# Agent attention with an expert layer, one core: score and routing products kept in program order behind the second-layer products, and a Square that waits for its buffer's transfer by step count

## The chip, the cores and the metric

The kernel runs on one core of a Trainium2 chip. Its time is the device time of one launch in microseconds (us); less is better. The engines are named as the profile names them: PE (TensorE, matrix products; its weight loads have a row of their own, PEld), DVE (VectorE), ACT (ScalarE), POOL (GpSimd) and SP (SyncE, which here only issues DMA transfers). Each engine works through its own list of instructions in order.

## The reference, cut to what matters

Four batches of 11456 tokens with 128 channels. A softmax over the keys pools the values into 49 agent rows, a softmax over the agents gives every token its attention output x. Then a layer with eight experts: each token goes to the expert with the largest cosine to x, through two matrix products with a Relu between, times its gate.

```python
a2k = sm(agents, k)          # softmax over the 11456 keys
agent_v = a2k @ v            # 49 x 128
q2a = sm(q, agents)          # softmax over the 49 agents
x = q2a @ agent_v            # what the experts see
...
logits = xn @ en.T / tau     # xn, en: normalised rows
expert_idx = np.argmax(logits, axis=1)
...
h = np.maximum(x[mask] @ w1[e], 0.0)
out[mask] = gate_w[mask, None] * (h @ w2[e])
```

## The kernel before, in words

Nearly all tokens of a batch choose one expert. The kernel picks that expert per batch, runs the layer densely for it, and mends the few strays at the end.

A **tile** is 512 tokens (128 partitions by 4 columns), a **unit** is two tiles; a batch has 12 units, the last of 192 tokens. The inner width of 1024 is cut into eight blocks of 128, so there are 184 **steps** a batch and 736 in all, one for each (batch, tile, block). A step is:

- `ffn_mm1`: two products of 512 columns into the PSUM tile `hp` (L723, L724; `gh` and `gl` are the high and low half of the first weights, folded with the attention's values, `tt` the transposed softmax weights of the tokens), then on ACT the Relu into `hh` (L727) and on DVE the remainder `hl` (L728). `hp` has four buffers, and one is free again when `hl` is done.
- `ffn_mm2`, for the step four earlier (`LAG = 4`): 12 products of 128 columns into `yp` (L745 to L747).

Between the steps, generators prepare what later steps need; they hand over after a number of steps, and the numbers in their calls say how many. For each unit of keys and of queries `split` makes two halves in 16 bits: a Square on ACT (L299), three small instructions on DVE for a scale, a scaled copy on ACT (L303) into the buffer `xs` (named `ks` or `qs`), two instructions on POOL (L304, L305), and a DMA that transposes `xs` into `xT` (`kT` or `qT`, L307, issued from SP). `xs` and `xT` have `XB = 5` buffers each, shared by keys and queries. `scores` (L316 to L318) makes 24 small products of a unit into `sp`. For queries follow, in `q_unit`: the exponential (L578), two 16-bit halves `e` on ACT (L582) and POOL (L583), a transposing DMA into `tt` (L591), and the **routing products** `rtp` (L600, L601, 16 a unit), from which ACT takes `rtg` and `rt`. Values of the next batch are multiplied into `avp` (L406).

The keys of batch b+1 are split while batch b runs its steps; units of keys come about every 12 steps, units of queries every 16.

The program's text is only a proposal: a scheduler then writes each engine's list, and it may move an instruction ahead of others that stand before it in the text when, by its own estimates, that one could start earlier; `tc.high_priority(200)` lets `ffn_mm1` go ahead. The list is fixed when the kernel is built. On the chip an engine then follows its list, and waits where the next entry's operands aren't ready.

Of the kernel before, what the change touches and what calls it, by code (L numbers as in the profile page):

```python
# [3 lines left out]

# [26 lines left out]
def kernel(ctx: ExitStack, tc: tile.TileContext, q, k, v, agents, emb, tau, w1, w2, out):  # L31
# [24 lines left out]
    XB = 5  # L56
# [28 lines left out]


    ffn_at = [None]
    units = {}

    def tshape(t):  # L90
# [199 lines left out]

    def split(kind, b, u, g):

        s = units[kind, b, u]
        p, n = ushape(u)
        sq = sm.tile([P, 1], F32, name="usq", tag=kind + "usq", bufs=3)[:p]
        xs = wk.tile([P, UJ, 2, D], F16, name=kind + "s", tag="xs", bufs=XB)
        act.activation(xs[:p, :n, 0], s[:p, :n], AF.Square, accum_out=sq)  # L299
        yield g  # L300
        hs = half_scale(sq, 14, kind + "u", 4, *([qbias] if kind == "q" else []))
        sc, iv = yield from hs
        act.activation(xs[:p, :n, 0], s[:p, :n], AF.Copy, scale=sc)  # L303
        pool.tensor_tensor(out=s[:p, :n], in0=s[:p, :n], in1=sc.unsqueeze(2).broadcast_to([p, n, D]), op=ALU.mult)  # L304
        pool.tensor_tensor(out=xs[:p, :n, 1], in0=s[:p, :n], in1=xs[:p, :n, 0], op=ALU.subtract)  # L305
        xT = wk.tile([P, 2 * UJ, P], F16, name=kind + "T", tag="xT", bufs=XB)
        sp.dma_start_transpose(out=xT[:, : 2 * n, :p], in_=xs[:p, :n].rearrange("p c h d -> p (c h d)"))  # L307
        return xT, iv

    def scores(b, u, xT):  # L310
        p, n = ushape(u)
        s = pss("sp")
        for c in range(n):
            o = s[:p, c * A : (c + 1) * A]
            hi, lo = xT[:, 2 * c, :p], xT[:, 2 * c + 1, :p]
            pe.matmul(out=o, lhsT=hi, rhs=a16[:, b, :A], start=True, stop=False)  # L316
            pe.matmul(out=o, lhsT=hi, rhs=a16[:, b, A:], start=False, stop=False)
            pe.matmul(out=o, lhsT=lo, rhs=a16[:, b, :A], start=False, stop=True)  # L318
        return s[:p, : n * A].rearrange("p (c a) -> p c a", a=A)


# [233 lines left out]
    def q_unit(b, u, g):  # L555
        bt = batches[b]
        p, n = ushape(u)
        while ("q", b, u) not in units:
            yield 1
        f32 = b == 0 and u < QF  # L560
        if f32:
            xT = pe_T(units["q", b, u], p, n)
            yield 1
            s = pss("sp")
            for c in range(n):
                pe.matmul(out=s[:p, c * A : (c + 1) * A], lhsT=xT[:, c * p : (c + 1) * p], rhs=aT_all[:, b, :], start=True, stop=True)
            spv = s[:p, : n * A].rearrange("p (c a) -> p c a", a=A)
            iv = SCALE
        else:
            xT, iv = yield from split("q", b, u, g[0])  # L570
            yield g[1]
            spv = scores(b, u, xT)
        mx = sm.tile([P, UJ], F32, name="qmx", tag="qmx")[:p, :n]
        dve.tensor_reduce(out=mx, in_=spv, axis=AX.X, op=ALU.max)
        e = wk.tile([P, UJ, A], F32, name="qe", tag="qe", bufs=LEAD)[:p, :n]
        dve.tensor_tensor(out=e, in0=spv, in1=mx.unsqueeze(2).broadcast_to([p, n, A]), op=ALU.subtract)
        yield g[2]
        act.activation(e, e, AF.Exp, scale=iv)  # L578
        yield g[3]
        e2 = e16[u % len(e16)]  # L580
        hi = e2[:p, :n, :A]
        act.copy(hi, e)  # L582
        (dve if f32 else pool).tensor_tensor(out=e2[:p, :n, LO : LO + A], in0=e, in1=hi, op=ALU.subtract)  # L583
        tt = wk.tile([P, UJ * P], F16, name="tt", tag="tt", bufs=LEAD + 2)
        if f32:
            tp = psh("tp").bitcast(F16)
            for c in range(n):
                pe.transpose(out=tp[:, c * p : (c + 1) * p], in_=e2[:p, c, :], identity=ident16[:p, :p])
            act.copy(tt[:, : n * p], tp[:, : n * p])
        else:  # L590
            sp.dma_start_transpose(out=tt[:, : n * p].rearrange("k (c p) -> k c p", p=p),  # L591
                                   in_=e2[:p, :n, :].rearrange("p c k -> p (c k)"))
        yield g[4]
        tts[b, u] = tt
        while not hasattr(bt, "r_hi"):
            yield 1
        s = (pss if ffn_at[0] else psh)("rtp")
        for c in range(n):
            o = s[:p, c * RW : (c + 1) * RW]
            pe.matmul(out=o, lhsT=tt[:, c * p : (c + 1) * p], rhs=bt.r_hi, start=True, stop=False)  # L600
            pe.matmul(out=o, lhsT=tt[:, c * p : (c + 1) * p], rhs=bt.r_lo, start=False, stop=True)  # L601
        gi = group_of[u]
        us = groups[gi]
        if u == us[0]:
            rtgs[b, gi] = (wk.tile([P, GC, E + 1], F32, name="rtg", tag="rtg", bufs=4),
                           wk.tile([P, GC], F32, name="quad", tag="quad", bufs=4))
        rtg, quad = rtgs[b, gi]
        c0 = ucol(u) - ucol(us[0])
        cs = slice(c0, c0 + n)
        if p < P:  # L610
            pool.memset(rtg[p:, cs], 1.0)
            pool.memset(quad[p:, cs], 1.0)
        sv = s[:p, : n * RW].rearrange("p (c w) -> p c w", w=RW)
        rt = wk.tile([P, UJ, A], F32, name="rt", tag="rt", bufs=1)[:p, :n]
        act.copy(rtg[:p, cs], sv[:, :, : E + 1])  # L615
        act.copy(rt, sv[:, :, E + 1 :])
        pool.tensor_tensor(out=rt, in0=rt, in1=e, op=ALU.mult)
        yield g[5]
        dve.tensor_reduce(out=quad[:p, cs], in_=rt, axis=AX.X, op=ALU.add)
        if u == us[-1]:  # L620
            spawn(route_group(b, gi, c0 + n), 1, half=True)
# [92 lines left out]
    def ffn_mm1(i):  # L714
        b, t, f = ffn_steps[i]
        bt = batches[b]
        u, w = unit_of(t)
        p, n = tshape(t)
        m = p * n
        tt = tts[b, u][:, w * TJ * P : w * TJ * P + m]  # L720
        hp = psh("hp")
        fs = slice(f * P, (f + 1) * P)
        pe.matmul(out=hp[:, :m], lhsT=bt.gh[:, fs], rhs=tt, start=True, stop=False)  # L723
        pe.matmul(out=hp[:, :m], lhsT=bt.gl[:, fs], rhs=tt, start=False, stop=True)  # L724
        hh = wk.tile([P, TJ * P], F16, name="hh", tag="hh", bufs=LAG + 2)
        hl = wk.tile([P, TJ * P], F16, name="hl", tag="hl", bufs=LAG + 2)
        act.activation(hh[:, :m], hp[:, :m], AF.Relu)  # L727
        dve.scalar_tensor_tensor(out=hl[:, :m], in0=hp[:, :m], scalar=0.0, in1=hh[:, :m], op0=ALU.max, op1=ALU.subtract)  # L728
        live[i] = (hh, hl)

    def ffn_mm2(i):

        b, t, f = ffn_steps[i]
        bt = batches[b]
        p, n = tshape(t)
        hh, hl = live.pop(i)
        if f == 0:
            yps[b, t] = psy("yp").rearrange("p (c d) -> p c d", d=D)
        yp = yps[b, t]

        for c in range(n):
            y = yp[:p, c, :]
            cs = slice(c * p, (c + 1) * p)
            last = f == NF - 1 and c == n - 1
            pe.matmul(out=y, lhsT=hh[:, cs], rhs=bt.w2h[:, f, :], start=(f == 0 and c == 0), stop=False, skip_group_check=True)  # L745
            pe.matmul(out=y, lhsT=hh[:, cs], rhs=bt.w2l[:, f, :], start=False, stop=False, skip_group_check=True)  # L746
            pe.matmul(out=y, lhsT=hl[:, cs], rhs=bt.w2h[:, f, :], start=False, stop=last, skip_group_check=True)  # L747

    def ffn_out(b, t):

# [181 lines left out]


    active = []
    now = [0]

    def spawn(g, at=0, half=False):
        t0 = now[0] + (now[0] % 2)
        active.append([t0 + 2 * at, g, 1 if half else 2])
# [71 lines left out]
    def keys():  # L1011
# [12 lines left out]
        for i, (at, kind, b, u) in enumerate(ops):  # L1024
# [4 lines left out]
            if kind == "k":  # L1029
                if not hasattr(batches[b], "blks"):  # L1030
                    k_start(b)
                spawn(k1_unit(b, u, (1, 7)))
            else:
                kb = batches[b].blks[0]
                if u == 0:
                    while kb.k1 < NU:
                        yield 1
                    yield from k_max(b, pss, 1)
                    yield 1
                spawn(k2_unit(b, u, pool, (3, 4)))  # L1040
                if u == NU - 1:
                    spawn(after_keys(b))
# [6 lines left out]
    def queries():  # L1049
        for b in range(B):  # L1050
            for u in range(NU):
                if b == 0 and u < LEAD:
                    continue
                for i in (b * NU + u, b * NU + u + 1):
                    unit_load(q, "q", i // NU, i % NU)
                spawn(q_unit(b, u, (1, 7, 1, 1, 6, 2)), 3)
                yield UT * NF if u < NU - 1 else NF

    def step2(i):
# [70 lines left out]
```

## Time and profile before

| | us |
|---|---|
| median of 3 runs (1103.6 to 1106.59) | 1105.27 |
| the profiled execution | 1101.58 |
| its span, first to last instruction | 1099.8 |
| PE busy, of 13878 products | 1019.3 (93%) |
| DVE busy | 770.5 (70%) |
| ACT busy | 724.2 (66%) |
| POOL busy | 580.1 (53%) |

The first 100 us load, and score batch 0's keys; the 736 steps then run from 101 us to the end. A row of the waits reads: engine, tile and line of the one that waited, arrow, engine, tile and line of the one it waited for, then total us, times and the longest. A row of the timeline reads: start, duration, engine, line, operation, output and inputs, and in brackets the idle time before it and who ended it. A row of windows reads: from and to, length, and for each engine its busy us and instructions, then the clock that was granted to PE as a share, the mean busy share of the DMA engines, and GB/s.

### The profile page before, as it was taken

The numbers are of one execution on the slowest core, as the hardware profiler recorded it, in microseconds if no ns is written. First come the engines' busy times: TensorE is split into PE (matmuls) and PEld (weight loads), VectorE is DVE, ScalarE is ACT, GpSimd is POOL, SyncE is SP. The second block draws the span as 40 slices with busy tenths as digits, with TensorE's granted clock in tenths as the row PEclk, the third lists the DMA queues.
The fourth block names the chain that finished last, engine by engine and source line by source line (L and its number), as shares of the span: only waits on it lengthen the run. The fifth ranks groups of instructions, "written<-read, shape, count | busy, mean of one in ns | idle before, by whom it ended". The sixth has DMA issues, their size and how long they took to land.

```text
span 1099.8 us, 33877 instructions
## 1 busy us (share of the span) xinstructions
PE 1019.3 (93%) x13878; PEld 809.8 (74%) x13878; DVE 770.5 (70%) x1779; ACT 724.2 (66%) x1406; POOL 580.1 (53%) x653
## 2 busy tenths in 40 slices
PE   7876979999998898999999988999999989999997
PEld 7764767777776777777777766777777767877776
DVE  5665757666786677766686766766677778777785
ACT  3456978777559787766648866675556856755553
POOL 2334998786516987764524985544321835532300
PEclk9777999999999999999999999999999999999999
DMA  9549899956339988744436997452113524631101
GB/s 335 151 100 280 182 227 233 229 167 119 85 66 282 231 189 188 167 117 89 94 82 225 224 229 144 92 110 69 31 41 138 100 61 119 123 83 40 42 30 35
DMA packets 283944, 152.63 MB, mean 139 GB/s; under 512 B 208315, under 2 KB 260619, under 8 KB 283787
## 3 DMA queue, kind: packets, MB, share of 16 engines
q1 hardware_dynamic: 270603, 126.98, 51.2%
q10 hardware_dynamic: 13120, 23.47, 5.9%
q8 instruction: 109, 1.79, 0.7%
q14 instruction: 48, 0.39, 0.1%
q0 software_dynamic: 64, 0.00, 0.0%
HBM read 75.80 MB, written 23.53 MB: 90 GB/s over the span
## 4 chain that ended last, share of the span: by engine, by line
PE 53%; DMA 13%; POOL 13%; issue 9%; ACT 6%; DVE 5%; SPq 1%; ACTq 0%; POOLq 0%; DVEq 0%
PE hp L723 9%; PE yp L745 8%; PE yp L747 8%; PE hp L724 8%; PE yp L746 8%; DMA kT<-ks 4%; DMA tt<-e 4%; PE avp L406 4%; DMA qt<-in_q_dram 3%; POOL qs L305 2%; POOL qt L304 2%; POOL ks L305 2%; ACT hh L727 2%; POOL kt L304 2%; PE sp L380 2%
## 5 line engine op out<-in xcount | busy, mean ns | idle before, releaser
L728 DVE SCALAR_TENSOR_TENSOR hl<-hp,hh 128x512 f16<-128x512 f32 (+1 forms) x736 | 480.8, 671 | 142.5 <-ACT hh L727 121.7
L727 ACT ACTIVATE hh<-hp 128x512 f16<-128x512 f32 (+1 forms) x736 | 416.8, 588 | 186.1 <-PE yp L746 78.8
L745 PE MATMUL yp<-w2h,hh 128*128 128x128 f16 (+1 forms) x2880 | 522.4, 220 | 9.1 <-ACT hh L727 8.1
L746 PE MATMUL yp<-w2l,hh 128*128 128x128 f16 (+1 forms) x2880 | 521.7, 220 | 0.7 <-DVE w2l L532 0.7
L747 PE MATMUL yp<-w2h,hl 128*128 128x128 f16 (+1 forms) x2880 | 521.0, 220 | 0.0
L745 PEld LDWEIGHTS <-hh 128*128 128x128 f16 (+1 forms) x2880 | 285.3, 99 | 63.3 <-ACT hh L727 12.8
L747 PEld LDWEIGHTS <-hl 128*128 128x128 f16 (+1 forms) x2880 | 285.0, 99 | 47.2 <-issue 1.1
L746 PEld LDWEIGHTS <-hh 128*128 128x128 f16 (+1 forms) x2880 | 285.0, 99 | 42.1 <-issue 3.7
L723 PE MATMUL hp<-tt,gh 128*128 128x512 f16 (+1 forms) x736 | 275.9, 375 | 22.4 <-DVE hl L728 21.2
L724 PE MATMUL hp<-tt,gl 128*128 128x512 f16 (+1 forms) x736 | 276.0, 375 | 0.0
L304 POOL TENSOR_TENSOR qt<-qt,hsc 128x1024 f32<-128x1024 f32 (+1 forms) x46 | 81.8, 1781 | 49.6 <-ACT qs L303 42.9
L724 PEld LDWEIGHTS <-gl 128*128 128x128 f16 x736 | 72.0, 98 | 31.3 <-issue 28.7
L305 POOL TENSOR_TENSOR qs<-qt,qs 128x1024 f16<-128x1024 f32 (+1 forms) x46 | 92.0, 2004 | 0.4
L304 POOL TENSOR_TENSOR kt<-kt,hsc 128x1024 f32<-128x1024 f32 (+1 forms) x36 | 64.4, 1788 | 31.2 <-ACT ks L303 31.1
L723 PEld LDWEIGHTS <-gh 128*128 128x128 f16 x736 | 72.2, 98 | 8.5 <-issue 5.9
L650 POOL TENSOR_SCALAR l<-rtg 128x16 f32<-128x16 f32 (+2 forms) x28 | 8.2, 293 | 133.1 <-ACT rtg L615 132.4
L583 POOL TENSOR_TENSOR e<-qe,e 128x392 f16<-128x392 f32 (+1 forms) x46 | 39.7, 863 | 69.4 <-ACT e L582 58.7
L305 POOL TENSOR_TENSOR ks<-kt,ks 128x1024 f16<-128x1024 f32 (+1 forms) x36 | 72.8, 2022 | 0.6
L299 ACT ACTIVATE qs<-qt 128x1024 f16<-128x1024 f32 (+1 forms) x46 | 46.3, 1008 | 35.5 <-DMA qT<-qs 14.7
L648 POOL TENSOR_TENSOR nrm<-quad,half 128x16 f32<-128x16 f32 (+2 forms) x28 | 68.2, 2434 | 1.8
L406 PE MATMUL avp<-vt,kd 128*64 128x129 f32 x720 | 62.1, 297 | 6.5 <-issue 4.3
L760 DVE TENSOR_TENSOR ot<-yp,gs 128x512 f32<-128x512 f32 (+1 forms) x92 | 61.4, 670 | 9.6 <-PE yp L747 8.8
(264 smaller groups left out, 1452.7 us busy)
## 6 DMA issues: line engine op xcount, KB each, us to landing
kt<-in_k_dram SPq DMA_DIRECT2D x44, 512.0 KB, 5.9
qt<-in_q_dram SPq DMA_DIRECT2D x44, 512.0 KB, 6.2
vt<-in_v_dram SPq DMA_DIRECT2D x44, 512.0 KB, 5.2
out_dram<-ot ACTq DMA_DIRECT2D x88, 256.0 KB, 2.4
w1s<-in_moe_w_dram SPq DMA_DIRECT2D x5, 512.0 KB, 3.9
w2s<-in_moe_w_dram SPq DMA_DIRECT2D x5, 512.0 KB, 4.9
qT<-qs SPq DMA_TRANSPOSE x46, 5.0
tt<-e SPq DMA_TRANSPOSE x46, 3.5
```

What stands on the lines that cost most here:

```text
L304: pool.tensor_tensor(out=s[:p, :n], in0=s[:p, :n], in1=sc.unsqueeze(2).broadcast_to([p, n, D]), op=ALU.mult)
L305: pool.tensor_tensor(out=xs[:p, :n, 1], in0=s[:p, :n], in1=xs[:p, :n, 0], op=ALU.subtract)
L406: pe.matmul(out=avp[hs, :W], lhsT=de[:p, c * A : c * A + LO], rhs=src[:p, c, :], start=(c < 2), stop=(c >= n - 2), skip_group_check=True)
L648: pool.tensor_tensor(out=nrm, in0=quad[:, :n], in1=half[:, :n], op=ALU.pow)
L723: pe.matmul(out=hp[:, :m], lhsT=bt.gh[:, fs], rhs=tt, start=True, stop=False)
L724: pe.matmul(out=hp[:, :m], lhsT=bt.gl[:, fs], rhs=tt, start=False, stop=True)
L727: act.activation(hh[:, :m], hp[:, :m], AF.Relu)
L728: dve.scalar_tensor_tensor(out=hl[:, :m], in0=hp[:, :m], scalar=0.0, in1=hh[:, :m], op0=ALU.max, op1=ALU.subtract)
L745: pe.matmul(out=y, lhsT=hh[:, cs], rhs=bt.w2h[:, f, :], start=(f == 0 and c == 0), stop=False, skip_group_check=True)
L746: pe.matmul(out=y, lhsT=hh[:, cs], rhs=bt.w2l[:, f, :], start=False, stop=False, skip_group_check=True)
L747: pe.matmul(out=y, lhsT=hl[:, cs], rhs=bt.w2h[:, f, :], start=False, stop=last, skip_group_check=True)
L760: dve.tensor_tensor(out=o[:p, :n], in0=yp[:p, :n], in1=gate, op=ALU.mult)
```

## The change

Three things, all in which entry stands where; each engine keeps exactly the instructions that it had.

1. `scores` and the routing products are wrapped in `tc.issue_after(y_last)`: in PE's list they stay behind the last second-layer product that the program's text has made so far.
2. A Square is wrapped in `tc.issue_after(h_last)`, and so stays in ACT's list behind the last Relu that the text has made so far. Besides, `split` holds its generator back until the transfer of the unit five earlier, which used the same `xs` buffer, was written into the program at least `XT = 6` steps ago.
3. Numbers of steps: the scores follow the split 8 steps later and not 7; a query unit starts at 2 and not 3 steps; its routing products come 8 steps after its transfer and not 6.

```diff
+    y_last, h_last, xs_at = [], [], []
+    XT = 6
+
+    def in_place(last):
+        return tc.issue_after(last[-1].ins) if last else nullcontext()
 
     def split(kind, b, u, g):
...
+        while ffn_at[0] and len(xs_at) >= XB and not (xs_at[-XB] and now[0] >= xs_at[-XB] + 2 * XT):
+            yield 1
+        i = len(xs_at)
+        xs_at.append(0)
         sq = sm.tile([P, 1], F32, name="usq", tag=kind + "usq", bufs=3)[:p]
         xs = wk.tile([P, UJ, 2, D], F16, name=kind + "s", tag="xs", bufs=XB)
-        act.activation(xs[:p, :n, 0], s[:p, :n], AF.Square, accum_out=sq)
+        with in_place(h_last):
+            act.activation(xs[:p, :n, 0], s[:p, :n], AF.Square, accum_out=sq)
...
         sp.dma_start_transpose(out=xT[:, : 2 * n, :p], in_=xs[:p, :n].rearrange("p c h d -> p (c h d)"))
+        xs_at[i] = now[0]
...
     def scores(b, u, xT):
...
-        for c in range(n):
+        with in_place(y_last):
+            for c in range(n):
...
         s = (pss if ffn_at[0] else psh)("rtp")
-        for c in range(n):
+        with in_place(y_last):
+            for c in range(n):
...
-        act.activation(hh[:, :m], hp[:, :m], AF.Relu)
+        h_last[:] = [act.activation(hh[:, :m], hp[:, :m], AF.Relu)]
...
-            pe.matmul(out=y, lhsT=hl[:, cs], rhs=bt.w2h[:, f, :], start=False, stop=last, skip_group_check=True)
+            y_last[:] = [pe.matmul(out=y, lhsT=hl[:, cs], rhs=bt.w2h[:, f, :], start=False, stop=last, skip_group_check=True)]
...
-                spawn(k1_unit(b, u, (1, 7)))
+                spawn(k1_unit(b, u, (1, 8)))
...
-                spawn(q_unit(b, u, (1, 7, 1, 1, 6, 2)), 3)
+                spawn(q_unit(b, u, (1, 8, 1, 1, 8, 2)), 2)
```

Up to the first steps the lists are the same (the first 668 entries of PE, 82 of ACT). Three places show what moves after that. In the lists of the changed kernel the line numbers are higher by some: Relu L744, Square L313, scaled copy L317, scores L332 to L334, transposes L321 and L607, first layer L740 and L741, second layer L762 to L764.

ACT, around the 162nd to 167th Relu, near the end of batch 0. Before, Squares (`qs,usq` and `ks,usq`), scaled copies (`qs<-qt,hsc`, `ks<-kt,hsc`) and the copy of the next expert's weights (`w2h`) stand two and three between one Relu and the next:

```order
L299 ACTIVATE qs,usq<-qt 128x8x128
L299 ACTIVATE ks,usq<-kt 128x8x128
L727 ACTIVATE hh<-hp 128x512
L662 ACTIVATE ex<-lga 128x64
L727 ACTIVATE hh<-hp 128x512
L299 ACTIVATE ks,usq<-kt 128x8x128
L303 ACTIVATE qs<-qt,hsc 128x8x128
L727 ACTIVATE hh<-hp 128x512
L529 ACTIVATE w2h<-w2s,hsc 128x1024
L299 ACTIVATE qs,usq<-qt 128x8x128
L303 ACTIVATE ks<-kt,hsc 128x8x128
L727 ACTIVATE hh<-hp 128x512
```

The same Relus after the change:

```order
L313 ACTIVATE ks,usq<-kt 128x8x128
L744 ACTIVATE hh<-hp 128x512 x2
L485 COPY av_all<-avsT 49x128
L744 ACTIVATE hh<-hp 128x512
L317 ACTIVATE ks<-kt,hsc 128x8x128
L545 ACTIVATE w2h<-w2s,hsc 128x1024
L744 ACTIVATE hh<-hp 128x512
L537 ACTIVATE gh<-gp,sgw 128x512
L783 DMA out_dram<-ot 128x512
L537 ACTIVATE gh<-gp,sgw 128x512
L744 ACTIVATE hh<-hp 128x512 x4
```

Six Squares and scaled copies stood in the rows before, two stand in the rows now; the other units' Squares come up to tens of steps later, one unit at a time.

PE, the scores of the seventh unit of batch 1's keys, before (`LDWEIGHTS` is a weight load; `gh` and `gl` are the first layer's weights):

```order
L723 LDWEIGHTS gh
L723 MATMUL hp<-tt,gh 128x512
L724 LDWEIGHTS gl
L724 MATMUL hp<-tt,gl 128x512
L316 LDWEIGHTS kT
L316 MATMUL sp<-a_132,kT 128x49
L317 LDWEIGHTS kT
L317 MATMUL sp<-a_132,kT 128x49
```

and after:

```order
L762 LDWEIGHTS hh
L762 MATMUL yp<-w2h,hh 128x128
L763 LDWEIGHTS hh
L763 MATMUL yp<-w2l,hh 128x128
L332 LDWEIGHTS kT
L332 MATMUL sp<-a_132,kT 128x49
L333 LDWEIGHTS kT
L333 MATMUL sp<-a_132,kT 128x49
```

The scores stood right behind a first-layer pair, and stand now behind second-layer products; both are at the 37th step.

SP, in batch 2's last steps and the start of batch 3, where only queries are left, before (`qT` is a unit's transpose, `tt` the transpose ahead of the routing products):

```order
L114 DMA qt<-in_q_dram 128x1024 x4
L591 DMA_TRANSPOSE tt<-e_1_152 128x8x128
L307 DMA_TRANSPOSE qT<-qs 128x16x128 x4
L591 DMA_TRANSPOSE tt<-e_0_151 128x8x128
L591 DMA_TRANSPOSE tt<-e_1_152 128x8x128
```

and after:

```order
L115 DMA qt<-in_q_dram 128x1024 x4
L321 DMA_TRANSPOSE qT<-qs 128x16x128
L607 DMA_TRANSPOSE tt<-e_1_152 128x8x128
L607 DMA_TRANSPOSE tt<-e_0_151 128x8x128
L321 DMA_TRANSPOSE qT<-qs 128x16x128
L607 DMA_TRANSPOSE tt<-e_1_152 128x8x128
```

Four units' transposes stood in a row ahead of the next `tt`; now they take turns.

More of the change, by code (lines that the diff above doesn't have):

```diff
@@ L2 @@
 from itertools import count
-from contextlib import ExitStack
+from contextlib import ExitStack, nullcontext
 import concourse.bass as bass
@@ L87 @@
     ffn_at = [None]
+    now = [0]
     units = {}
@@ L312, in scores @@
         s = pss("sp")
-        for c in range(n):
[L314 to L318, printed above, removed]
+        with in_place(y_last):
+            for c in range(n):
+                o = s[:p, c * A : (c + 1) * A]
+                hi, lo = xT[:, 2 * c, :p], xT[:, 2 * c + 1, :p]
+                pe.matmul(out=o, lhsT=hi, rhs=a16[:, b, :A], start=True, stop=False)
+                pe.matmul(out=o, lhsT=hi, rhs=a16[:, b, A:], start=False, stop=False)
+                pe.matmul(out=o, lhsT=lo, rhs=a16[:, b, :A], start=False, stop=True)
         return s[:p, : n * A].rearrange("p (c a) -> p c a", a=A)
@@ L597, in q_unit @@
         s = (pss if ffn_at[0] else psh)("rtp")
-        for c in range(n):
-            o = s[:p, c * RW : (c + 1) * RW]
-            pe.matmul(out=o, lhsT=tt[:, c * p : (c + 1) * p], rhs=bt.r_hi, start=True, stop=False)
-            pe.matmul(out=o, lhsT=tt[:, c * p : (c + 1) * p], rhs=bt.r_lo, start=False, stop=True)
+        with in_place(y_last):
+            for c in range(n):
+                o = s[:p, c * RW : (c + 1) * RW]
+                pe.matmul(out=o, lhsT=tt[:, c * p : (c + 1) * p], rhs=bt.r_hi, start=True, stop=False)
+                pe.matmul(out=o, lhsT=tt[:, c * p : (c + 1) * p], rhs=bt.r_lo, start=False, stop=True)
         gi = group_of[u]
@@ L934 @@
     active = []
-    now = [0]
     def spawn(g, at=0, half=False):
```

## The prediction

> **What bounds the kernel now.** I read the busy times first, then PE's busy time by stretch, then who PE waits for, then who holds up the engine that it waits for, and last the timeline at the longest waits.
>
> ```profile
> PE 1019.3 (93%) x13878; PEld 809.8 (74%) x13878; DVE 770.5 (70%) x1779; ACT 724.2 (66%) x1406; POOL 580.1 (53%) x653
> ```
>
> ```profile
> 0.00:100.00 100.00, 74.42 (x652) 68.59 (x653) 57.55 (x147) 43.17 (x80) 28.10 (x54) 0.80 0.68 200
> 100.00:1075.00 975.00, 925.68 (x12949) 724.32 (x12949) 698.58 (x1597) 671.88 (x1308) 551.96 (x600) 0.99 0.58 135
> 1075.00:1100.00 25.00, 19.21 (x278) 16.89 (x276) 14.34 (x37) 9.11 (x20) 0.00 (x0) 0.97 0.11 38
> ```
>
> ```profile
> 100.00:125.00 25.00, 20.30 (x267) 14.30 (x267) 17.86 (x50) 24.39 (x46) 22.65 (x21) 0.93 0.99 275
> 150.00:175.00 25.00, 20.03 (x286) 15.39 (x284) 15.49 (x36) 18.36 (x36) 22.89 (x21) 0.93 1.13 243
> 600.00:625.00 25.00, 21.77 (x306) 17.66 (x305) 16.62 (x40) 21.68 (x43) 25.00 (x18) 0.93 0.95 204
> 675.00:700.00 25.00, 20.03 (x280) 16.20 (x276) 14.92 (x31) 13.23 (x27) 9.87 (x11) 0.86 0.76 143
> 1000.00:1025.00 25.00, 25.00 (x355) 19.80 (x353) 17.86 (x28) 14.22 (x27) 3.72 (x8) 1.00 0.20 54
> ```
>
> PE bounds it. In the steps' stretch, 100 to 1075 us, PE idles 975 - 925.68 = 49.3 us; a change of order can only win that, and what a slowed clock costs. Where preparation is over (1000 to 1025 us) PE is full at clock 1.00, so the loss isn't in the steps but in what is prepared between them. The first 100 us stay: the lists are the same there.
>
> ```profile
> PE hp L723 <- DVE hl L728: 21.2, 34, 5.0
> PE rtp L600 <- DMA tt<-e: 11.4, 14, 2.2
> PE yp L745 <- ACT hh L727: 8.1, 10, 1.9
> PE sp L316 <- DMA kT<-ks: 3.5, 3, 1.8
> ...
> PE sp L316 <- DMA qT<-qs: 1.1, 1, 1.1
> ```
>
> These waits, taken in that stretch, make 45.3 of the 49.3 us. 29.3 of them (hp and yp) are Relus that came late, 11.4 routing products that wait for `tt`, 4.6 scores that wait for a transpose. ACT's own waits in the same stretch say why Relus come late:
>
> ```profile
> ACT qs L299 <- DMA qT<-qs: 14.7, 7, 6.3
> ACT qs L299 <- DMA qt<-in_q_dram: 9.3, 6, 2.5
> ...
> ACT qs L299 <- DMA kT<-ks: 8.0, 6, 3.1
> ...
> ACT gh L508 <- DMA w1s<-in_moe_w_dram: 5.2, 3, 3.5
> ACT ks L299 <- DMA kT<-ks: 5.0, 6, 1.8
> ACT ks L299 <- DMA qT<-qs: 4.4, 3, 1.9
> ```
>
> A Square (L299) writes `xs`, which an earlier unit's transpose must have left: 14.7 + 8.0 + 5.0 + 4.4 = 32.1 us of ACT's time, with Relus queued behind. The longest, on ACT and then on PE:
>
> ```profile
> 682.38 1.06 ACT L299 ACTIVATE qs<-qt 128x1024 f16<-128x1024 f32 x1 [6.32 <-DMA qT<-qs]
> ```
>
> ```profile
> 684.79 0.58 PE L723 MATMUL hp<-tt,gh 128*128 128x512 f16 x1 [4.97 <-DVE hl L728]
> ```
>
> Without any wait, Squares and scaled copies also bunch ahead of Relus, as here, at the Relus of the first order excerpt:
>
> ```profile
> 342.04 1.14 ACT L303 ACTIVATE qs<-qt,hsc 128x1024 f16<-128x1024 f32 x1
> 343.07 0.58 ACT L727 ACTIVATE hh<-hp 128x512 f16<-128x512 f32 x1
> 343.55 1.14 ACT L529 ACTIVATE w2h<-w2s,hsc 128x1024 f16<-128x1024 f32 x1
> 344.59 1.05 ACT L299 ACTIVATE qs<-qt 128x1024 f16<-128x1024 f32 x1
> 345.54 0.20 ACT L299 ACTIVATION_READ_ACCUMULATOR qs<-qt 128x1 f32 x1
> 345.63 1.14 ACT L303 ACTIVATE ks<-kt,hsc 128x1024 f16<-128x1024 f32 x1
> 346.67 0.58 ACT L727 ACTIVATE hh<-hp 128x512 f16<-128x512 f32 x1
> ```
>
> Two Relus start 3.6 us apart there.
>
> **The change, part by part.** No instruction is added or dropped; all is place.
>
> *Squares behind Relus, and spread (hp and yp, 29.3 us).* Counted in the two lists, the Squares and scaled copies between the 162nd and the 170th Relu fall from ten to two, at 1.05 to 1.14 us each; the same bunch stands near steps 345 and 529. The lead from a unit's scaled copy to its scores was 30 to 100 steps for most units and is now 10 to 19, so five buffers are never all taken when a Square comes: units come about seven steps apart, so a buffer is used again after some 30, and the 32.1 us have no cause left. For the same reason the wait by step count will hardly ever hold a generator back after the first steps; I give it nothing. What is late next: the expert's weights at a batch's end (5.2 us of ACT's waits on `w1s`), loads (9.3 us on `qt`), and ACT itself at the start, 24.39 of 25 us busy at 100 to 125 us. I take 20 of 29.3 as won. Ends: 5, which is the one wait of 4.97 above, and all 29.3.
>
> *Routing products (11.4 us).* One stall shows the mechanism: four units' transposes stood on SP ahead of a `tt`.
>
> ```profile
> 862.15 18.18 SPq L307 DMA_TRANSPOSE qT<-qs  x4
> 880.43 1.71 SPq L591 DMA_TRANSPOSE tt<-e  x1
> ```
>
> ```profile
> 884.06 0.20 PE L600 MATMUL rtp<-r_hi,tt 128*128 128x58 f16 x1 [2.18 <-DMA tt<-e]
> ```
>
> In the new list they take turns, and the routing products stand two steps later in the text. From the 16-bit cast to the first product the lists give 5 to 22 steps before and 6 to 11 mostly now, with two units at 4. I take 6 of 11.4 as won, half, since transposes still share a queue with loads. Ends: 5 lost (the 14 waits grow by a third of a us each) and 11.4 won.
>
> *Scores (4.6 us).* The path from scaled copy to transpose, by its rows:
>
> ```profile
> L304 POOL TENSOR_TENSOR qt<-qt,hsc 128x1024 f32<-128x1024 f32 (+1 forms) x46 | 81.8, 1781 | 49.6 <-ACT qs L303 42.9
> L305 POOL TENSOR_TENSOR qs<-qt,qs 128x1024 f16<-128x1024 f32 (+1 forms) x46 | 92.0, 2004 | 0.4
> ...
> L583 POOL TENSOR_TENSOR e<-qe,e 128x392 f16<-128x392 f32 (+1 forms) x46 | 39.7, 863 | 69.4 <-ACT e L582 58.7
> ```
>
> ```profile
> qT<-qs SPq DMA_TRANSPOSE x46, 5.0
> tt<-e SPq DMA_TRANSPOSE x46, 3.5
> ```
>
> 1.14 + 1.78 + 2.00 + 5.0 = 9.9 us. A step is 1.14 us or more (22 steps started at 1000 to 1025 us):
>
> ```profile
> 1000.00:1025.00 25.00, 8.33 (x22) 2.09 (x22) 1.00 0.20 54
> ```
>
> The usual lead of 12 steps is thus at least 13.7 us, 3.8 more than the path. In the first 60 steps POOL is nearly full (22.65 of 25), and there the leads got shorter (17 to 25, now 14 to 18): what is won later may be lost here. I take 1 us as won. Ends: 8 lost, 0.8 us for each of ten units of batch 1's keys, and 4.6 won.
>
> *The clock.* The four windows with a granted clock of 0.93, 0.93, 0.93 and 0.86 lack 0.07 + 0.07 + 0.07 + 0.14 of 25 us, so 8.75 us of full clock, each beside PE's waits. If two thirds of the waits go, I take 5.5; ends 0 and 8.75. The Trainium skill, "TensorE: Matmul & The Clock Gate", "What's actually happening", puts the half clock after at least one idle window of about 3.4 us. By that rule only the dip after the 4.97 us wait would go, and this term would be 25 x 0.14 = 3.5. The trace differs: three windows dip with no wait of PE above 2.2 us, so I stay with the rows.
>
> *What the pins cost.* A score or routing product can no longer fill PE while a second-layer product ahead of it waits; yp's waits, 8.1 us, bound what such filling is worth. Where the lead is 4 steps, 4 x 1.14 = 4.6 us stand against 0.86 + 3.5 for `e` and `tt`, and one 1.78 us `qt` ahead on POOL: 6.1, so 1.5 us short, twice. I take 5 lost; ends 0 and 12.
>
> **The sum.** 20 + 6 + 1 + 5.5 - 5 = 27.5 us. The profiled execution would go from 1101.58 to 1074.1, its span from 1099.8 to 1072.3. The median of the runs stands 3.7 above the profiled one, so 1105.27 - 27.5 = 1077.8, say 1078. With all good ends, 29.3 + 11.4 + 4.6 + 8.75 = 54, it would be 1051; with all bad ones, 5 - 5 - 8 + 0 - 12 = -20, it would be 1125.
>
> **Rivals.**
> - *PE waits for its own small products.* A product whose operand is late now holds everything behind it, and nearly all leads are cut to 12 steps or so. The slack of 3.8 us goes when two units' pairs on POOL meet (1.78 + 2.00 more), which happens where units of keys and queries come together. Against it: POOL has 551.96 of 975 us, and leads of 6 to 10 steps to `tt` cost 14 waits of 0.8 us before. It decides when the mean wait over some 75 groups of scores and 46 of routing products, about 120, passes 32.5 / 120 = 0.27 us above today's (32.5 is the sum without the pins' 5); at 0.4 the loss is 48, so 1105 - 32.5 + 48 = 1121. Slower.
> - *ACT stays the bound.* The bunch is thinner, but ACT's sum is the same, 671.88 us; if only the longest waits go (6.3, 3.1 and 1.9 of ACT, 2.2 of PE, of which PE gets about 8), it is 1097.
> - *Nearly every stall goes,* as in 1000 to 1025 us: 1105.27 - 49 = 1056.
> - *The pins change nothing that PE feels,* since the step four back (`LAG`) gives PE slack for either order: within 0.3%, 1105. Against it: 29.3 us of late Relus despite that slack.
>
> **How the numbers follow.** The forecast with a gain of 12 to 45 us, 1060 to 1093: 0.70. ACT stays the bound, a gain of 4 to 12: 0.08. Nearly every stall goes, under 1060: 0.07. No change: 0.06. Slower by its own small products: 0.09. A measurement here tells 0.3%, some 3.3 us, from no change. Faster is 0.70 + 0.08 + 0.07 = 0.85, same 0.06, slower 0.09. The range from 1058 to 1102 leaves out the slower case, the unchanged one and the best of the good one, just under 2 in 10.
>
> **What would show it.** Right: ACT's Squares have next to no wait on `qT` or `kT`; hp's wait on `hl` falls from 21.2 below 9; one clock dip is left at most beyond the start; SP shows no row of four `qT`. Wrong: rows of PE `rtp` on `tt` or `sp` on `kT` and `qT` above 15 us together; or ACT above 24 of 25 us in many windows with hp still waiting.

## The result, and the profile after

The changed kernel takes 1071.99 us (median of 4 runs, 1068.95 to 1074.95), the kernel before 1105.93 beside it (4 runs, 1103.6 to 1106.81). The ratio is 0.9696, with a 95% interval of 0.9664 to 0.9728. The profiled execution took 1072.67 us, with a span of 1070.9.

The busy times of the page, and the windows of the changed kernel (from and to, length, then busy us and instructions of PE, PEld, DVE, ACT and POOL, the granted clock, the DMA share and GB/s):

```profile
PE 1008.5 (94%) x13878; PEld 806.6 (75%) x13878; DVE 769.5 (72%) x1779; ACT 722.6 (67%) x1406; POOL 583.8 (55%) x653
```

```profile
0.00:100.00 100.00, 75.35 (x652) 69.17 (x653) 56.83 (x144) 41.62 (x77) 28.17 (x54) 0.80 0.68 197
100.00:1050.00 950.00, 917.89 (x13000) 723.62 (x13001) 701.36 (x1604) 673.92 (x1314) 555.67 (x600) 0.99 0.61 139
```

The first 100 us stayed (PE 75.35 us busy after, 74.42 before). In the steps' stretch PE idles 950 - 917.89 = 32.1 us, where it idled 49.3 (there the stretch ran to 1075). Who PE waits for there, all that is above 2 us:

```profile
PE sp L332 <- DMA kT<-ks: 18.2, 8, 5.7
PE rtp L617 <- DMA tt<-e: 3.7, 3, 1.8
PE sp L332 <- DMA qT<-qs: 3.0, 4, 1.8
PE hp L740 <- DVE hl L745: 3.0, 3, 2.2
PE rtp L617 <- DVE hiv L184: 2.1, 1, 2.1
```

Late Relus (hp on `hl`, yp on `hh`) fell from 29.3 us to 3.0; no row of yp on `hh` is left. Routing products fell from 11.4 to 3.7. The scores' waits for a transpose rose from 4.6 to 21.2, nearly all on `kT`, the transposed keys, in eight waits. ACT's waits in the same stretch show why Relus come in time: the longest row is now ACT waiting for PE, the first that names a transfer is the expert's weights, and no row has a Square (L313) waiting for a transfer:

```profile
ACT hh L744 <- PE yp L764: 86.3, 99, 3.6
...
ACT gh L524 <- DMA w1s<-in_moe_w_dram: 5.1, 3, 2.4
```

The clock did not recover. These are the windows of 25 us between 100 and 1050 us whose granted clock is below 0.97:

```profile
100.00:125.00 25.00, 21.73 (x296) 15.40 (x297) 20.02 (x52) 24.33 (x47) 22.34 (x21) 0.93 1.03 290
325.00:350.00 25.00, 19.34 (x280) 15.09 (x279) 17.03 (x42) 18.87 (x37) 20.20 (x22) 0.90 1.09 266
350.00:375.00 25.00, 24.37 (x350) 20.25 (x348) 18.41 (x43) 19.13 (x40) 18.52 (x18) 0.96 0.74 144
400.00:425.00 25.00, 22.44 (x307) 17.56 (x308) 15.89 (x33) 15.42 (x33) 8.56 (x10) 0.93 0.48 122
650.00:675.00 25.00, 23.38 (x318) 18.26 (x319) 15.92 (x31) 15.82 (x31) 8.56 (x10) 0.93 0.53 127
```

They lack 0.07 + 0.10 + 0.04 + 0.07 + 0.07 = 0.35 of 25 us, 8.75 us, as the four windows did before. That the two sums are equal is chance: in a second profile of the changed kernel the same sum was 12.25. The dips near 350, 400 and 650 stand beside the three longest waits for `kT`.

**Where those waits come from.** SP's queue and PE's timeline at the longest of them, and POOL's row that finishes `ks`, the unit that is to be transposed:

```profile
332.84 2.14 POOL L319 TENSOR_TENSOR ks<-kt,ks 128x1024 f16<-128x1024 f32 x1
```

```profile
329.42 1.09 SPq L115 DMA_DIRECT2D kt<-in_k_dram  x1
330.60 0.58 SPq L115 DMA_DIRECT2D qt<-in_q_dram  x1
331.23 1.00 SPq L115 DMA_DIRECT2D kt<-in_k_dram  x2
332.28 0.51 SPq L115 DMA_DIRECT2D qt<-in_q_dram  x1
332.84 1.13 SPq L115 DMA_DIRECT2D kt<-in_k_dram  x1
334.08 0.45 SPq L115 DMA_DIRECT2D qt<-in_q_dram  x1
335.01 7.68 SPq L321 DMA_TRANSPOSE kT<-ks  x1
```

```profile
347.99 0.22 PE L332 MATMUL sp<-a,kT 128*128 128x49 f16 x1 [5.66 <-DMA kT<-ks]
```

`ks` is ready at 332.84 + 2.14 = 334.98, and the transpose goes out at once. But seven loads went out in the 5.6 us before it, issuing it holds SP for 7.68 us, and its operand reaches PE 13 us after the issue began. The median transpose of `qT` lands after 5.0, that of `kT` after 6.0. Over the 78 transposes of `kT` and `qT` beyond the first 100 us the median time for which one holds SP grows with the loads issued in the 6 us before it: 1.8 us with none, 3.0 with one, 3.9 with two, 7.4 with four or more (six cases). The DMA engines have no slack there either (their mean busy share reads 1.30 from 335 to 343 us), so these rows don't tell a wait in SP's queue from a wait for the DMA engines. The second kind has only one load ahead: two units meet on POOL.

```profile
386.56 2.13 POOL L319 TENSOR_TENSOR qs<-qt,qs 128x1024 f16<-128x1024 f32 x1
388.65 1.89 POOL L318 TENSOR_TENSOR kt<-kt,hsc 128x1024 f32<-128x1024 f32 x1
390.62 2.13 POOL L319 TENSOR_TENSOR ks<-kt,ks 128x1024 f16<-128x1024 f32 x1
```

```profile
392.78 3.78 SPq L321 DMA_TRANSPOSE kT<-ks  x1
```

```profile
402.56 0.20 PE L332 MATMUL sp<-a,kT 128*128 128x49 f16 x1 [3.67 <-DMA kT<-ks]
```

The keys' pair on POOL had to follow the queries' `qs`, and the transpose left only at 392.78. It was slow besides: it landed 9.7 us after its issue.

**Why the span fell more than the idle time.** Over the whole span PE's idle time fell by 18.1 us (from 1099.8 - 1019.3 = 80.5 to 1070.9 - 1008.5 = 62.4), the span by 28.9. The other 10.8 us came off PE's busy time, with the same 13,878 products. The timeline of a full stretch shows how:

```profile
1009.88 0.22 PE L762 MATMUL yp<-w2h,hh 128*128 128x128 f16 x1
1009.94 0.22 PE L763 MATMUL yp<-w2l,hh 128*128 128x128 f16 x1
```

A product is recorded for 0.22 us, but the next starts some 0.06 us after it. Of every stop behind such a product the first 0.16 us therefore reads as busy. I counted instead from start to start, as what exceeds the median spacing of the same pair of neighbours by more than 0.15 us, beyond the first 100 us:

| first product after the stop | before | changed | Squares' place alone |
|---|---|---|---|
| hp and yp (late Relus) | 44.4 | 6.4 | 9.5 |
| rtp (routing products) | 14.0 | 4.2 | 18.9 |
| sp (scores) | 5.2 | 24.3 | 3.8 |
| others | 0.7 | 1.8 | 2.8 |
| sum, us (stops) | 64.3 (94) | 36.8 (38) | 35.0 (40) |

The sum fell by 27.5 us, which covers nearly all of the 28.9; with the neighbours grouped in other ways it falls by 26 to 29. The count also takes in products of 512 columns that ran at half the clock, 0.43 us apart instead of 0.22, without any stop: 1.6 us before, 2.6 in the changed kernel, 1.0 in the last column. The last column belongs to the first experiment.

### The profile page after: what moved, and what is told of

Read it like the earlier page. It is cut to its first block, busy times and chain, and to the rows that moved or that the text cites. A ratio compares the mean times of both kernels' runs of the same rounds, so it can differ in the third digit from the quotient of the medians.

```text
span 1070.9 us, 33823 instructions
## 1 busy us (share of the span) xinstructions
PE 1008.5 (94%) x13878; PEld 806.6 (75%) x13878; DVE 769.5 (72%) x1779; ACT 722.6 (67%) x1406; POOL 583.8 (55%) x653
## 4 chain that ended last, share of the span: by engine, by line
PE 71%; DMA 10%; DVE 5%; POOL 5%; ACT 4%; issue 3%; SPq 0%; ACTq 0%; POOLq 0%; DVEq 0%
PE yp L762 12%; PE hp L740 12%; PE yp L764 11%; PE yp L763 11%; PE hp L741 11%; DMA kT<-ks 5%; PE avp L422 5%; DMA qT<-qs 2%; PE sp L396 2%; ACT hh L744 1%; PE sp L332 1%; DMA tt<-e 1%; PE fTp L378 1%; PE sp L333 1%; PE sp L334 1%
## 5 line engine op out<-in xcount | busy, mean ns | idle before, releaser
L744 ACT ACTIVATE hh<-hp 128x512 f16<-128x512 f32 (+1 forms) x736 | 419.0, 591 | 225.1 <-PE yp L764 89.6
L762 PE MATMUL yp<-w2h,hh 128*128 128x128 f16 (+1 forms) x2880 | 519.2, 220 | 0.0
L764 PE MATMUL yp<-w2h,hl 128*128 128x128 f16 (+1 forms) x2880 | 518.7, 219 | 0.0
L762 PEld LDWEIGHTS <-hh 128*128 128x128 f16 (+1 forms) x2880 | 284.6, 99 | 45.7 <-issue 6.1
L764 PEld LDWEIGHTS <-hl 128*128 128x128 f16 (+1 forms) x2880 | 284.0, 99 | 39.3 <-issue 0.5
L740 PE MATMUL hp<-tt,gh 128*128 128x512 f16 (+1 forms) x736 | 276.6, 376 | 3.0 <-DVE hl L745 3.0
L741 PE MATMUL hp<-tt,gl 128*128 128x512 f16 (+1 forms) x736 | 276.5, 376 | 0.0
L740 PEld LDWEIGHTS <-gh 128*128 128x128 f16 x736 | 72.2, 98 | 7.5 <-issue 6.6
L741 PEld LDWEIGHTS <-gl 128*128 128x128 f16 x736 | 72.2, 98 | 5.9 <-issue 5.2
L318 POOL TENSOR_TENSOR kt<-kt,hsc 128x1024 f32<-128x1024 f32 (+1 forms) x36 | 64.3, 1786 | 22.3 <-ACT ks L317 22.0
L422 PEld LDWEIGHTS avp<-vt,kd 128*64 128x64 f32 x720 | 44.2, 144 | 23.2 <-issue 17.3
L634 POOL TENSOR_TENSOR rt<-rt,qe 128x392 f32<-128x392 f32 (+1 forms) x48 | 47.1, 981 | 26.5 <-ACT rt L633 25.6
```

Of the source, the lines that this page charges most:

```text
L422: pe.matmul(out=avp[hs, :W], lhsT=de[:p, c * A : c * A + LO], rhs=src[:p, c, :], start=(c < 2), stop=(c >= n - 2), skip_group_check=True)
L744: h_last[:] = [act.activation(hh[:, :m], hp[:, :m], AF.Relu)]
L764: y_last[:] = [pe.matmul(out=y, lhsT=hl[:, cs], rhs=bt.w2h[:, f, :], start=False, stop=last, skip_group_check=True)]
```

## The experiments

Theory A: the gain is the Squares' place on ACT. They no longer wait there for a buffer with Relus queued behind, and no longer bunch. Theory B, the rival: the gain comes from the products kept back on PE, the step numbers or the wait by step count. Theory M, on the loss: the scores wait for `kT` because loads stand ahead of its transpose on SP.

Some answers need no run. Built with the Squares' place, the product pins and the wait by step count change no entry: the changed kernel without either of them has the same list on all five engines, entry for entry. So has the kernel before with the Squares' place alone beside the one with the pins and the wait added. With the Squares free, too, pins and wait change no entry once the new numbers of steps are in. So the changed kernel is the Squares' place and the numbers of steps, nothing else. What is left to test is the Squares' place, the pins without it, and the numbers of steps. In the kernels below line numbers shift by a few.

**The Squares' place alone.** The kernel before, and this:

```diff
-        act.activation(xs[:p, :n, 0], s[:p, :n], AF.Square, accum_out=sq)
+        with in_place(h_last):
+            act.activation(xs[:p, :n, 0], s[:p, :n], AF.Square, accum_out=sq)
```

> The kernel before with one thing alone: a Square stays behind the last Relu of the text (no pins of products, no wait by step count, old numbers of steps). Theory A, that the Squares' place on ACT is the gain: hp and yp waits of PE together fall from 29.3 to under 6 us, ACT's Squares wait for no transpose, time 1073 to 1083, since the scores and routing products keep the shorter leads. Theory B, that the later scores and routing products are the gain: hp and yp stay above 20 us and the time above 1095.

It took 1068.0 us against 1103.26, a ratio of 0.9686 (0.9659 to 0.9713). PE's waits in the steps' stretch:

```profile
PE rtp L615 <- DMA tt<-e: 16.9, 12, 3.6
PE hp L738 <- DVE hl L743: 5.1, 7, 2.1
...
PE sp L330 <- DMA qT<-qs: 1.3, 3, 0.8
PE sp L330 <- DMA kT<-ks: 1.3, 3, 0.6
```

The one pin brings the whole gain, with a time below the 1073 to 1083 us expected, and late Relus fall nearly as far; no row of ACT has a Square waiting for a transpose. The pin moves more than Squares, since the scheduler writes what follows them anew: counted in the lists, a unit's scaled copy now stands 9 to 27 steps ahead of its scores, where it stood 10 to 101. The numbers of steps only decide who waits for a transpose: routing products here (16.9), scores there (21.2).

**The change without the Squares' place.** The changed kernel, with the Square free:

```diff
-        with in_place(h_last):
+        with nullcontext():
             act.activation(xs[:p, :n, 0], s[:p, :n], AF.Square, accum_out=sq)
```

> The changed kernel with the Square's pin taken off; pins of products, wait by step count and new numbers of steps stay. Theory A: ACT's Squares wait again some 25 to 35 us for transposes, hp and yp are above 20 us, time 1092 to 1106. Theory B: the gain stays, under 1080, with hp and yp near 3 us.

It took 1098.32 us, a ratio of 0.9952 (0.9925 to 0.9979): about 5 us remain of the gain, from the numbers of steps, since pins and wait move nothing here. The Squares wait for transposes as they did before, 30.5 us in these rows of ACT (32.1 before), and PE's late Relus are 17.1 us:

```profile
ACT qs L313 <- DMA qT<-qs: 11.5, 7, 3.6
...
ACT qs L313 <- DMA kT<-ks: 7.4, 4, 3.4
...
ACT ks L313 <- DMA kT<-ks: 6.2, 7, 1.8
ACT ks L313 <- DMA qT<-qs: 5.4, 3, 2.6
```

```profile
PE hp L740 <- DVE hl L745: 14.3, 20, 2.5
...
PE yp L762 <- ACT hh L744: 2.8, 5, 0.9
```

That is less than the 20 us expected at least, and less than the 29.3 before, though ACT's waits are nearly the same. The time gained less than these waits: in this profile the windows between 100 and 1050 us lack 17.25 us of clock, where 8.75 were lacking before.

**The product pins alone.** The kernel before, with only `scores` and the routing products in `tc.issue_after(y_last)`; about 50 entries of PE's list differ:

```diff
-        for c in range(n):
+        with in_place(y_last):
+            for c in range(n):
```

> The kernel before with only the score and routing products kept behind the second-layer products; Squares free, old step numbers. Only about 50 entries of PE's list stand elsewhere. If the gain is the Squares' place on ACT, this stays within 0.5% of the kernel before (about 1100 to 1109 us) and PE's waits for late Relus (hp and yp together) stay between 20 and 35 us. If keeping the products back helps by itself, it gains 5 us or more; if it costs what the prediction took (5 us, up to 12), it is 0.4 to 1% slower, with hp, sp or rtp waits longer by that much.

It took 1103.39 us against 1102.7, a ratio of 1.0006 (0.998 to 1.0032). The waits are those of before:

```profile
PE hp L738 <- DVE hl L743: 19.8, 30, 4.3
PE rtp L615 <- DMA tt<-e: 12.1, 15, 2.2
PE yp L760 <- ACT hh L742: 7.0, 11, 1.5
```

The pins neither help nor cost. With the two runs above, Theory B has fallen but for the 5 us that the numbers of steps bring where the Squares are free.

**Keys' scores later.** The changed kernel, 10 steps instead of 8:

```diff
-                spawn(k1_unit(b, u, (1, 8)))
+                spawn(k1_unit(b, u, (1, 10)))
```

> The changed kernel, with scores of keys 10 steps after the split and not 8. Theory L, that the 18.2 us in which scores wait for a transpose of keys are a lead too short, since two units' pairs meet on POOL: two steps, 2.3 us, come off each of the four longest waits (5.7, 4 and so on), sp's waits fall from 21.2 to about 11, and time falls by 5 to 12 us. Theory M, that a row of loads ahead on the queue is the cause: the two waits at the start of a batch (about 5.7 and 1.8 us) stay, only the other two fall, time falls by 0 to 5 us.

The wait of the scores on `kT` fell from 18.2 to 9.4 us, and the time did not: 1071.57 us, a ratio of 0.9723 (0.9692 to 0.9754). PE's busy time rose to 1012.7.

```profile
PE sp L332 <- DMA kT<-ks: 9.4, 6, 2.7
```

The waits came out by Theory L (11.3 with those on `qT`, and the 5.7 at the start of batch 1 is gone), the time by Theory M (0 to 5 us less), so the run decides for neither. A wait that gets shorter need not shorten the kernel.

**Routing products later.** The Squares' place alone, and one number:

```diff
-                spawn(q_unit(b, u, (1, 7, 1, 1, 6, 2)), 3)
+                spawn(q_unit(b, u, (1, 7, 1, 1, 8, 2)), 3)
```

> The kernel before with only the Squares kept behind Relus, and of the step numbers only one changed: routing products 8 steps after their transfer instead of 6 (the Squares alone, with 6, took 1068.0 and left rtp waiting 16.9 us for tt, scores 2.6 for kT and qT). If the waits of rtp and of the scores are separate, each set by its own number, rtp's fall below 6, the scores' stay below 6, and the time is 1055 to 1063. If SP's queue only hands the same lateness from one to the other, the scores' waits rise by about what rtp's lose and the time stays at 1066 to 1073.

It took 1069.74 us, a ratio of 0.9692 (0.9661 to 0.9722): nearer the second answer, though the scores' waits rose by twice what the routing products' lost.

```profile
PE rtp L615 <- DMA tt<-e: 11.0, 12, 1.7
PE sp L330 <- DMA kT<-ks: 10.5, 6, 3.9
PE sp L330 <- DMA qT<-qs: 4.2, 5, 1.8
```

The routing products' wait lost 5.9 us and the scores' gained 12.1, though no number of theirs had moved. What they share are SP's queue and the DMA engines behind it, and the numbers set the order there; which of the two passes the lateness on is not shown.

**Loads behind transposes.** The changed kernel, with each load kept on SP behind the last transpose that the text has made:

```diff
-        sp.dma_start(out=s[:p, :n, :D], in_=src)
+        with (tc.issue_after(t_last[-1].ins) if t_last and ffn_at[0] else nullcontext()):
+            sp.dma_start(out=s[:p, :n, :D], in_=src)
...
-        sp.dma_start_transpose(out=xT[:, : 2 * n, :p], in_=xs[:p, :n].rearrange("p c h d -> p (c h d)"))
+        t_last[:] = [sp.dma_start_transpose(out=xT[:, : 2 * n, :p], in_=xs[:p, :n].rearrange("p c h d -> p (c h d)"))]
```

(and the same at the transpose ahead of the routing products).

> The changed kernel, with each load kept on SP behind the last transpose of the text, so that no row of six or seven loads stands ahead of a transpose of keys. Theory M: the issue of 7.7 us and the wait of 5.7 at the start of batch 1 go, and with them the half clock there; sp's waits fall from 21.2 to 8 to 14 us and the time by 5 to 12 us. Theory L: sp's waits stay at 18 us or more, the time within 3 us; loads that now come later could hold Squares, which would show as ACT waits on loads and cost some us.

It took 1063.65 us, a ratio of 0.9632 (0.9598 to 0.9667). The wait on `kT` fell to 4.8 us with 1.5 as the longest, and no window between 125 and 1050 us had a low clock; the wait on `qT` rose to 11.7.

```profile
PE sp L334 <- DMA qT<-qs: 11.7, 12, 1.7
PE sp L334 <- DMA kT<-ks: 4.8, 9, 1.5
```

Theory M is borne out for the long waits. As a sum the scores' waits fell only to 16.5 us, between the two theories. The lack of clock fell from 8.75 us to 1.75, and from 12.25 to 5.25 in the profiles of the side-by-side runs below: 7.0 us in both, most or all of what the span gained there (8.2 and 5.6 us). The same edit on the kernel with the routing products at 8 steps says how far it goes:

> The same as the run above (Squares behind Relus, routing products at 8 steps, other numbers old), and each unit's load kept on SP behind the last transpose of the text. If the loads ahead of transposes cost PE time beside what the step number costs, this is 3 to 8 us faster than that run, near 1055, with rtp and score waits together below 10 us and no half-clock window between 110 and 1050 us. If the step number alone had already removed the waits, it is within 3 us of it.

That took 1070.43 us (0.9707, 0.9651 to 0.9764), no better than 1069.74 without the edit, with its four runs spread from 1063.5 to 1074.28. The scores kept 15.3 us of waits:

```profile
PE sp L332 <- DMA qT<-qs: 8.3, 7, 2.8
PE sp L332 <- DMA kT<-ks: 7.0, 5, 2.4
PE rtp L617 <- DMA tt<-e: 2.5, 5, 0.8
```

**Loads behind transposes and all scores later,** 10 steps for keys and queries:

```diff
-                spawn(k1_unit(b, u, (1, 8)))
+                spawn(k1_unit(b, u, (1, 10)))
...
-                spawn(q_unit(b, u, (1, 8, 1, 1, 8, 2)), 2)
+                spawn(q_unit(b, u, (1, 10, 1, 1, 8, 2)), 2)
```

> The changed kernel, loads kept behind transposes (1063.65 before this run, with 11.7 us of waits for qT and 4.8 for kT left), and both keys' and queries' scores 10 steps after the split instead of 8. If PE's remaining waits for transposes cost the time that they show, they fall from 16.5 to below 5 and the time by 6 to 12 us, to 1052 to 1058. If later scores only crowd the steps behind them, the waits go but the time stays within 3 us of 1063.65, as it did with the keys alone at 10 steps.

It took 1061.13 us, a ratio of 0.9612 (0.9581 to 0.9643). The scores' waits went, and the routing products' came back:

```profile
PE rtp L619 <- DMA tt<-e: 10.9, 11, 2.0
PE total L192 <- ACT gh L526: 5.0, 3, 2.1
PE sp L334 <- DMA qT<-qs: 2.1, 2, 1.6
...
PE sp L334 <- DMA kT<-ks: 0.7, 1, 0.7
```

**Four of them side by side.** These differences are some tenths of a per cent, so four kernels ran again on one chip, in more rounds: the changed kernel, the Squares' place alone, the loads behind transposes, and the last one.

> The changed kernel once more, side by side with the three below on one chip. If the step numbers only move PE's waits from the routing products to the scores, it stays within 3 us of the Squares alone (next run). If the 21.2 us that the scores wait cost more than the 13.2 us that rtp saved, it is 4 us or more slower than the Squares alone.

> The kernel before with the Squares' place on ACT alone. Expected ratio 0.966 to 0.971 as in its first run (0.9686). The changed kernel's whole gain (0.9696) if nothing else in it counts.

> The changed kernel with each load kept on SP behind the last transpose of the text. If loads ahead of transposes cost PE time, it is 5 to 9 us faster than the changed kernel (8.3 in its first run). If that was the spread of the runs, as the run with routing products at 8 steps suggests, where keeping loads back gave nothing (1070.43 against 1069.74), it is within 3 us.

> The same with scores 10 steps behind the split for keys and queries. Expected 1059 to 1063; within 3 us of the run above if later scores only pass the wait on to the routing products (10.9 us there in its first run, 4.5 without), 5 us or more faster if the scores' waits count by themselves.

| kernel | us (6 runs) | ratio to before (1103.97) | 95% interval |
|---|---|---|---|
| changed | 1069.31 | 0.9677 | 0.9644 to 0.9710 |
| Squares' place alone | 1069.12 | 0.9678 | 0.9647 to 0.9709 |
| changed, loads behind transposes | 1064.35 | 0.9633 | 0.9606 to 0.9660 |
| the same, scores 10 steps later | 1061.51 | 0.9611 | 0.9585 to 0.9637 |

The changed kernel and the Squares alone are equal to 0.2 us. Keeping loads back is 5.0 us faster here and 8.3 in its first run (7 by the ratios, since the kernel before was 2.7 us faster beside that run), but the intervals still overlap a little. The last kernel's interval is clear of the changed kernel's: it is 7.8 us faster, and the fastest of all. What scores 10 steps later add to it, 2.5 to 2.8 us, is within the spread.

## Why the prediction was right, and where its terms were not

The forecast was 1078 us, in a range from 1058 to 1102; it came out at 1071.99. The main step held. Of the terms around it, the clock (5.5 us won) and the pins (5 lost) were both nothing and cancelled, and the scores came out with the wrong sign. By PE's wait rows the three terms for waits give 26.3 + 7.7 - 16.6 = 17.4 us, where the forecast had 27.5 and the span lost 28.9: the number is close because the price of a stop, read too small, made up for the scores. That nearness is luck; the step that carries the gain is not.

- **Squares behind Relus, taken at 20 of 29.3 us.** Right in kind and in place: the Squares' waits are gone, ACT no longer holds Relus up, and the Squares' place alone gives the whole gain. Its size was 26.3 us by PE's wait rows (29.3 to 3.0) and 38.0 by starts (44.4 to 6.4). The upper end, "all 29.3", was too low, since I took wait rows for the whole price of a stop. Whether the waits for buffers or the bunches mattered more was not separated: one pin removes both. The run with the Squares free has nearly the same buffer waits (30.5 us) with only 17.1 us of late Relus, so ACT's waits are no measure of what PE loses by them.
- **The wait by step count, given nothing.** Right: without it every list is the same.
- **Routing products, taken at 6 of 11.4 us.** They gained 7.7. But the cause given, that the new order lets transposes take turns, is only half of it: with the Squares' place alone they wait 16.9 us, so the Squares' place made them worse and the numbers of steps made them better.
- **Scores, taken as 1 us won, with an end of 8 lost.** This step failed: 16.6 us were lost. I had allowed 0.8 us for each of ten units of keys, as the mean of other waits, and set the lead of 13.7 us against a path of 9.9. The path's last part, 5.0 us, was a median; behind a row of loads the same transpose needed 13. A short lead alone doesn't make the loss: with the Squares' place alone the scores come one step sooner after the split, and wait 2.6 us for transposes; there the row of loads stood ahead of a transpose of queries, which held SP for 8.68 us at 324.81. The rival that PE waits for its own small products named the meeting of two units on POOL, and that happened near 390 us. It stayed a loss within a gain: all waits for transposes together rose from 16.0 us (11.4 + 4.6) to 24.9 (18.2 + 3.7 + 3.0), far from the 0.27 us in each of 120 groups that it needed.
- **The clock, taken at 5.5 us.** Nothing came: 8.75 us lack as before, and the new dips stand beside new waits of PE. With the Squares' place alone, without the scores' long waits, 3.5 us lacked in one profile and 7.0 in the other, where the changed kernel lacked 8.75 and 12.25. The Trainium skill, "TensorE: Matmul & The Clock Gate", "What's actually happening", ties the half clock to an idle window of about 3.4 us. Here the three dips after 340 us agree with it, beside waits of 5.66, 3.67 and 4.05 us. Another run does not: with loads behind transposes, in the run side by side, a window was granted 0.93 whose only wait of PE for a transfer was 1.91 us:

```profile
400.00:425.00 25.00, 23.09 (x315) 18.39 (x314) 17.49 (x37) 16.87 (x35) 9.20 (x14) 0.93 0.50 114
```

```profile
415.66 0.20 PE L334 MATMUL sp<-a,qT 128*128 128x49 f16 x1 [1.91 <-DMA qT<-qs]
```

- **The pins' cost, taken at 5 us.** It had no object. With the Squares' place the pins move nothing; alone they cost 0.06% in an interval from -0.2 to 0.3%.
- **The signs.** Of the four right ones, three came true (no Square waits, hp below 9, no row of four `qT`); "one clock dip at most" did not. The sign for wrong, rtp and sp above 15 us together, came true as well at 24.9 while the forecast held. It was set too low beside what the Relus gave back.

## What to carry to other kernels

When an engine off the bound has work with early operands and late ones in one queue, first look whether an early item waits there for a buffer while the bound engine's operand is queued behind it; here one such pin was worth 3.2%. Before numbers of steps are tuned, read which transfers share a queue: a number that frees one consumer hands the lateness to the next, and only the order in the queue, loads behind transposes, and later consumers together went beyond the pin. Price a stop of a pipelined engine by the starts of its instructions, since its idle time leaves out a part of each.

## What the runs showed of the hardware that was not expected

A transpose of `kT` by DMA that was issued behind seven loads of 96 to 512 KB held SP's queue for 7.68 us and reached its reader 13 us after its issue began; the median for `kT` was 6.0 us. Another, with four loads in the 2.3 us before it, held the queue for 7.70. Idle time understated what the stops had cost: 10.8 of the 28.9 us that the span lost read as busy, since a product that is recorded for 0.22 us is followed by the next after some 0.06.
